# Adding up the weighted values of attention by accumulating on-chip transfers instead of VectorE additions

## The chip, the cores and the metric

One Trainium2 chip, of which the kernel uses one core. The metric is the device time of one execution in microseconds (us), as the median of several runs; lower is better.

## The reference

The input `x` has 2048 rows of 640 numbers (float32). Its layer norm `xn` goes two ways, and the two results are combined:

```python
qkv = xn @ wqkv                        # 32 heads of 20 columns, each with q, k, v
# sliding window: row s looks at rows s, s-2, ..., s-14 (8 places)
logits = einsum("bhsd,bhswd->bhsw", q, kg) * scale    # masked where the row would be below 0
attn = softmax(logits, axis=-1)
o = einsum("bhsw,bhswd->bhsd", attn, vg)              # the sum that the change is about
s = o @ wo
g = silu(((xn @ w_gate) * (xn @ w_up)) @ w_down)
return x + s * g
```

The weights of both ways are scaled by 8. What the change touches is the second `einsum`: for each row, eight value vectors are weighted by the softmax and added.

## The kernel before, in words

**Products in split form.** Every large product is computed by TensorE from operands that are split into a high and a low part (`mm3`, L95; `qkv`, L295), three products for one. Weights are split as they are needed: ScalarE writes the high part (L85), GpSimd writes the low part by a subtraction (L86, `split_wf` for the gate and up weights, `split_wq` for the q, k, v weights).

**Units.** Attention is cut into 12 units: six groups of heads (four of 5 heads, two of 6) times even and odd rows. A unit has eight column blocks of 128 rows. `qkv(u, i)` makes block i on TensorE and ScalarE copies it out of PSUM into the unit's `q` and `kv` tiles (L297, L298). Transfers then shift `kv` rows from partition to partition (`kv<-kv`, L302), so that all eight places of the window lie in the same partition as the row.

**Attention of a unit** (`attention`, a Python generator, L306) is nearly all VectorE work. For each of four pairs of window places: a product of q and k (L329) and a sum over the 20 columns of a head (L332). Then the softmax: mask, maximum, subtraction (L336 to L339), the exponential on ScalarE (L341), sum, reciprocal, product (L343 to L345). Then, for each of four pairs, a product of weights and values (`weighted`, L350), where the first goes to the tile `acc` and the other three go to `t` and are added to `acc` (L358). One last addition joins the two halves of a pair (L361) into the tile `o`, which is stored to memory (`o_scr`, L366).

**Pieces.** Between the units, TensorE works on pieces of the gate and up products: `gate_up(f, ch)` multiplies 128 columns f of both weights with 512 rows ch. A piece is 15 matmuls into a PSUM bank `g` and 15 into a bank `u`, two banks of each. ScalarE copies `g` to `gs` (L397). While any unit's attention is under way, VectorE multiplies `u` with `gs` into `hs` (L408), which frees the bank `u`; else ScalarE copies `u` (L410) and GpSimd multiplies (L411). `hs` is stored (`h_scr<-hs`, L412). The instruction L408 of a piece is put into the program after the first half of the next piece.

**What sets the order.** All instructions stand in a fixed order on each engine. Attention's steps are woven between TensorE's by a budget: each `yield` of the generator names what it costs VectorE in us, and `advance` takes steps until the budget that TensorE's work has granted is used up. A unit's attention can begin only when its last `qkv` has been issued. When no unit is under way, the budget is set to zero.

**Buffers.** `t` has two buffers, for products of q and k and for weighted values alike; `acc` is one of them too. `e` and `o` have one buffer each.

Of the kernel before, what the change touches and what calls it, by code (L numbers as in the profile page):

```python
# [14 lines left out]
ALU = mybir.AluOpType  # L15
# [4 lines left out]
P = 128  # L20
S, D, F = 2048, 640, 1536
H, DH = 32, 20
W, DIL = 8, 2
NT = S // P
NE = NT // DIL
# [15 lines left out]
PAIRS = range(0, W, 2)  # L41
# [9 lines left out]
def kernel(  # L51
# [11 lines left out]
    nc = tc.nc  # L63
# [68 lines left out]
    def load_x(s, n, t, cuts=(0, D)):  # L132
        j = tile_column(s)
        for c0, c1 in zip(cuts, cuts[1:]):
            nc.sync.dma_start(t[:, :, c0:c1], (xbv if s < NE else xv)[:, j:j + DIL * (n - 1) + 1:DIL, c0:c1])  # L135
        for i in range(n):
            xt[s + i] = t[:, i, :]
# [8 lines left out]
    load_x(4, 4, xc[:, 0:4])  # L146
    load_wf(1)
    load_x(8, 4, xc[:, 4:8])
    xd = st([P, 1, D], "o", 1)
    load_x(14, 1, xa[:, 2:3])  # L150
    load_x(15, 1, xd)
    ident = st([P, P], "ident", 1)
# [12 lines left out]
    o_scr = dr.tile([DIL, NQ, NE, P, QC], F32, name="o_scr")  # L165
# [98 lines left out]
    UN = [(g, r) for g in range(len(GROUPS)) for r in range(DIL)]  # L264
# [41 lines left out]
    def attention(u):  # L306
        g, r = UN[u]
        nh = GROUPS[g]
        c = nh * DH
        q, kv = q_t[u], kv_t[u]  # L310
        pair, one, small = [(n + 155) / 950 for n in (2 * NE * c, NE * c, NE * nh * W)]
        lg = st([P, NE * nh, W], "lg", 2)
        e = st([P, NE * nh, W], "e", 1)
        yield 1.0

        def places(a, j):

            y = kv[:, a, j:j + NE, :].rearrange("p i c -> p (i c)")
            return bass.AP(y.tensor, y.offset, [y.ap[0], [c, 2], y.ap[1]])

        def pair_tile():
            return st([P, 2, NE * c], "t", 2)

        def heads(y):
            return y.rearrange("p a (n d) -> p a n d", d=DH)

        for j in PAIRS:
            t = pair_tile()
            nc.vector.tensor_mul(t, q.rearrange("p i c -> p (i c)").unsqueeze(1).to_broadcast([P, 2, NE * c]),  # L329
                                 places(0, j))  # L330
            yield pair
            nc.vector.tensor_reduce(out=lg[:, :, j:j + 2].rearrange("p n a -> p a n"), in_=heads(t),  # L332
                                    op=ALU.add, axis=AX.X)
            yield pair
        m0 = lg[0:1].rearrange("p (i h) w -> p i h w", h=nh)
        nc.vector.tensor_add(m0, m0, mask.unsqueeze(2).to_broadcast([1, NE, nh, W]))  # L336
        sm = st([P, 2, NE * nh], "sm", 2)
        nc.vector.tensor_reduce(out=sm[:, 0, :], in_=lg, op=ALU.max, axis=AX.X)
        nc.vector.tensor_sub(lg, lg, sm[:, 0, :].unsqueeze(2).to_broadcast([P, NE * nh, W]))  # L339
        yield 3 * small  # L340
        nc.scalar.activation(e, lg, AF.Exp, scale=SCALE)  # L341
        yield small
        nc.vector.tensor_reduce(out=sm[:, 0, :], in_=e, op=ALU.add, axis=AX.X)  # L343
        nc.vector.reciprocal(sm[:, 1, :], sm[:, 0, :])
        nc.vector.tensor_mul(e, e, sm[:, 1, :].unsqueeze(2).to_broadcast([P, NE * nh, W]))  # L345
        yield 3 * small

        def weighted(j, t):
            pw = e[:, :, j:j + 2].rearrange("p n a -> p a n").unsqueeze(3).to_broadcast([P, 2, NE * nh, DH])
            nc.vector.tensor_mul(heads(t), pw, heads(places(1, j)))  # L350

        acc, t = pair_tile(), pair_tile()
        weighted(PAIRS[0], acc)
        yield pair
        for j in PAIRS[1:]:
            weighted(j, t)
            yield pair
            nc.vector.tensor_add(acc, acc, t)  # L358
            yield pair
        o = st([P, NE, c], "o", 1)  # L360
        nc.vector.tensor_add(o.rearrange("p i c -> p (i c)"), acc[:, 0, :], acc[:, 1, :])  # L361
        yield one
        for b in range(NQ):
            c0, c1 = max(GOFF[g], b * QC), min(GOFF[g] + c, (b + 1) * QC)
            if c0 < c1:
                nc.sync.dma_start(o_scr[r, b, :, :, c0 - b * QC:c1 - b * QC].rearrange("s p c -> p s c"),  # L366
                                  o[:, :, c0 - GOFF[g]:c1 - GOFF[g]])

    running = []

# [85 lines left out]
    def load_o(s, n, t):  # L456


        for b in range(NQ):
            nc.sync.dma_start(t[b * QB:(b + 1) * QB].rearrange("i n (q c) -> i (n q) c", c=QC),  # L460
                              o_scr[s // NE, b, s % NE:s % NE + n].rearrange("n (q i) c -> i (n q) c", i=QB))
        for i in range(n):
            o_t[s + i] = t[:, i]
# [24 lines left out]
    KH = KF // 2  # L488
# [21 lines left out]
    def sum_wd(k, part):  # L510
        r = wd_raw[k]
        if part == 0:
            v = wd_v[k] = {"B11": r[:, 0, 0], "B21": r[:, 1, 0], "B22": r[:, 1, 1]}
            v["T1"], v["T2"] = st([P, HALF], "lg", 2), st([P, HALF], "lg", 2)
            nc.vector.tensor_sub(v["T1"], r[:, 0, 1], r[:, 0, 0])
            nc.vector.tensor_sub(v["T2"], r[:, 1, 1], v["T1"])
        else:
            v = wd_v[k]
            v["T4"], v["T3"] = st([P, HALF], "e", 1), r[:, 0, 1]
            nc.vector.tensor_sub(v["T3"], r[:, 1, 1], r[:, 0, 1])  # L520
            nc.vector.tensor_sub(v["T4"], r[:, 1, 0], v["T2"])

# [8 lines left out]
    def load_h(n):  # L531

        a, b = 2 * n, 2 * n + 1
        if n % 2:
            ta, tb = st([P, KF, P], "t", 2), st([P, KF, P], "t", 2)
            nc.sync.dma_start(ta, h_scr[a])
            nc.sync.dma_start(tb, h_scr[b])
            h_raw[n] = {"A11": ta[:, :KH], "A12": ta[:, KH:], "A21": tb[:, :KH], "A22": tb[:, KH:]}
        else:
            h_raw[n] = {}  # L540
            for name, s, k, tag, m in (("A11", a, 0, "wraw", 3), ("A21", b, 0, "wraw", 3),
                                       ("A22", b, KH, "wraw", 3), ("A12", a, KH, "o", 1)):
                h_raw[n][name] = st([P, KH, P], tag, m)
                nc.sync.dma_start(h_raw[n][name], h_scr[s][:, k:k + KH])

# [63 lines left out]
    def gather(m):  # L609

        n, j = divmod(m, 7)
        a, b = 2 * n, 2 * n + 1
        p = bank["ACACABA"[j]]
        if j == 0:
            keep("M1", p, "lg", 2)
        elif j == 1:
            keep("M5", p, "lg", 2)
        elif j == 2:
            keep("U2", p, "e", 1)
        elif j == 3:  # L620
            g_t[a] = st([P, D], "q", 2)
            nc.vector.tensor_add(g_t[a][:, HALF:], kept["U2"], p)
            return lambda: silu(a, 1)
        elif j == 4:
            g_t[b] = st([P, D], "q", 2)
            nc.vector.tensor_add(g_t[b][:, HALF:], kept["M5"], p)
            return lambda: silu(b, 1)
        elif j == 5:
            nc.vector.tensor_add(g_t[a][:, :HALF], kept["M1"], p)
            return lambda: silu(a, 0)  # L630
        else:
            return lambda: silu(b, 0, p)
        return lambda: None
# [26 lines left out]
    nc.gpsimd.memset(mask, 0.0)  # L660
    for i in range(NE - 1):
        nc.gpsimd.memset(mask[:, i, :W - 1 - i], MASKED)
    sel = st([P, NQ, P], "sel", 1)
    nc.gpsimd.tensor_copy(sel.rearrange("p q (b i) -> p q b i", i=QB),
                          ident.rearrange("p (q i) -> p q i", i=QB).unsqueeze(2).to_broadcast([P, NQ, NQ, QB]))
    norm(4, 4)
# [82 lines left out]
    for ch in range(NCH):  # L749
        gate_up(f0, ch)  # L750
        if ch == 0:
# [3 lines left out]
            t = load_wo((4,))  # L755
    for ch in range(NCH):
        if ch == 3:
            load_wd(0)
            trans_o(0)
            load_o(1, 1, st([P, 1, D], "o", 1))  # L760
            load_o(2, 3, st([P, 3, D], "t", 2))
            load_o(5, 3, st([P, 3, D], "t", 2))
        gate_up(f1, ch)
        if ch < 3:
            for k in ((0, 1), (2, 3), (4,))[ch]:
                split_wo(k)
        if ch == 1:
            drain(len(UN) - 2)
            load_o(0, 1, t[:, 1:2])
        if ch == 2:  # L770
            advance(1e9)
# [24 lines left out]
    load_sx(0)  # L796
    load_sx(1)
    load_h(1)
    AHEAD = 4
    sum_h(1)  # L800
# [4 lines left out]
    for m in range(n_prod):  # L805
        n, j = divmod(m, 7)
# [61 lines left out]
```

## Time and profile before

| what | value |
|---|---|
| time, median of 3 runs | 787.05 us (786.82 to 787.56) |
| the profiled execution, first to last instruction | 786.0 us |
| TensorE matmul (PE) busy | 778.0 us, 99% |
| VectorE (DVE) busy | 659.3 us, 84% |
| ScalarE (ACT) busy | 234.2 us, 30% |
| GpSimd (POOL) busy | 147.9 us, 19% |
| granted TensorE clock, mean | 0.999 |

The profiled execution has no total of its own beside its span; the timed runs lie 1.05 us above that span. In the rows of the profile, PE is TensorE's matmuls and PEld its weight loads, DVE is VectorE, ACT ScalarE, POOL GpSimd, and SP the engine that issues transfers. "L329" is line 329 of the kernel. A row of a timeline gives start and duration in us, engine, line, operation, and output<-input tiles. "x2" counts merged instructions. A time in brackets is idle time of the engine before the row and who ended it.

### The profile page before, as it was taken

What the parts mean: (1) busy time and instruction counts of PE and PEld (TensorE: products, weight loads), DVE (VectorE), ACT (ScalarE), POOL (GpSimd) and SP (SyncE); (2) the same over time, 40 slices, a digit from 0 to 9 for tenths busy, and PEclk for the clock granted to TensorE, in tenths of its full rate; (3) what the DMA queues carried; (4) which work ended last, traced back from release to release, by engine and by line L of the source; (5) the groups of instructions that cost most, each with busy time, mean ns of one, the idle gap of its engine ahead of it and who ended that gap; (6) DMA issues with size and microseconds to landing.
All of it is one profiled execution on the core that took longest, in us unless ns stands there. A gap on an engine that the chain in (4) does not pass through costs nothing.

```text
span 786.0 us, 11222 instructions
## 1 busy us (share of the span) xinstructions
PE 778.0 (99%) x4454; PEld 708.9 (90%) x4454; DVE 659.3 (84%) x660; ACT 234.2 (30%) x536; POOL 147.9 (19%) x110
## 2 busy tenths in 40 slices
PE   8999999999999999999999999999999999999997
PEld 6889898888898898899898989888899999999997
DVE  6889899999999979996999999992177667777775
ACT  5334211121112111311221202012366564444442
POOL 5301211022013200410231000112467600000000
PEclk9999999999999999999999999999999999999999
DMA  8172122141132321404033131332797574555534
GB/s 321 67 230 75 42 61 72 48 123 48 50 83 89 95 71 61 117 28 112 28 105 86 58 86 58 107 103 66 160 274 209 170 270 131 206 200 188 182 101 135
DMA packets 81661, 92.68 MB, mean 118 GB/s; under 512 B 23032, under 2 KB 63304, under 8 KB 81480
## 3 DMA queue, kind: packets, MB, share of 16 engines
q1 hardware_dynamic: 81608, 91.96, 38.2%
q8 instruction: 35, 0.57, 0.3%
q14 instruction: 18, 0.15, 0.1%
HBM read 54.53 MB, written 28.31 MB: 105 GB/s over the span
## 4 chain that ended last, share of the span: by engine, by line
PE 97%; DMA 2%; ACT 1%; DVE 0%; SPq 0%; POOL 0%; issue 0%
PE q L295 26%; PE u L95 21%; PE g L95 21%; PE q L606 11%; PE q L95 9%; PE u L606 5%; PE g L606 3%; DMA wraw<-in_wgu 1%; DMA wraw<-in_wqkv 1%; PE q L229 0%; ACT wf L85 0%; SPq L135 0%; ACT wqh L85 0%; ACT xc L230 0%; POOL wql L86 0%; PE q L249 0%
## 5 line engine op out<-in xcount | busy, mean ns | idle before, releaser
L95 PE MATMUL u<-xc,wf 128*128 128x512 f32 (+1 forms) x735 | 176.2, 390 | 0.0
L95 PE MATMUL g<-xc,wf 128*128 128x512 f32 (+1 forms) x735 | 176.1, 390 | 0.0
L95 PEld LDWEIGHTS u<-xc,wf 128*128 128x128 f32 x735 | 135.7, 187 | 32.2
L95 PEld LDWEIGHTS g<-xc,wf 128*128 128x128 f32 x735 | 135.3, 187 | 31.0
L295 PE MATMUL q<-wqh,xc 128*128 128x300 f32 (+1 forms) x960 | 159.8, 309 | 2.1 <-DVE xc L231 1.2
L295 PEld LDWEIGHTS q<-wqh,xc 128*128 128x128 f32 x960 | 146.0, 188 | 4.3 <-DVE xc L231 1.5
L329 DVE TENSOR_TENSOR t<-q,kv 128x1600 f32<-128x1600 f32 (+1 forms) x48 | 97.9, 2040 | 10.1 <-DMA kv<-kv 10.1
L350 DVE TENSOR_TENSOR t<-e,kv 128x1600 f32<-128x1600 f32 (+1 forms) x48 | 97.5, 2051 | 1.1
L86 POOL TENSOR_TENSOR wf<-wraw,wf 128x256 fp32r<-128x256 f32 (+2 forms) x22 | 48.8, 2232 | 248.1 <-ACT wf L85 248.1
L332 DVE TENSOR_REDUCE lg<-t 128x80 f32<-128x1600 f32 (+1 forms) x48 | 92.6, 1930 | 1.2
L397 ACT ACTIVATE gs<-g 128x512 f32<-128x512 f32 x48 | 28.7, 598 | 205.9 <-PE g L95 197.2
L295 PE MATMUL q<-wql,xc 128*128 128x300 f32 (+1 forms) x480 | 86.3, 309 | 0.0
L358 DVE TENSOR_TENSOR t<-t,t 128x1600 f32<-128x1600 f32 (+1 forms) x36 | 80.2, 2228 | 1.1
L295 PEld LDWEIGHTS q<-wql,xc 128*128 128x128 f32 x480 | 74.4, 188 | 0.0
L297 ACT ACTIVATE kv<-q 128x200 f32<-128x200 f32 (+1 forms) x96 | 33.4, 348 | 129.4 <-PE q L295 129.4
L606 PE MATMUL q<-xc,wf 128*128 128x320 f32 x432 | 67.3, 309 | 0.0
L606 PEld LDWEIGHTS q<-xc,wf 128*128 128x128 f32 x432 | 64.3, 188 | 0.0
L86 POOL TENSOR_TENSOR wql<-wraw,wqh 128x300 fp32r<-128x300 f32 (+4 forms) x15 | 34.0, 2292 | 142.7 <-ACT wqh L85 142.7
L95 PE MATMUL q<-wf,wf 128*128 128x320 f32 x156 | 35.7, 310 | 0.0
L408 DVE TENSOR_TENSOR hs<-u,gs 128x512 f32<-128x512 f32 x39 | 26.6, 683 | 0.6 <-issue 0.6
L95 PEld LDWEIGHTS q<-wf,wf 128*128 128x128 f32 x156 | 26.1, 188 | 0.0
L86 DVE TENSOR_TENSOR wf<-ot,wf 128x640 fp32r<-128x640 f32 x13 | 15.5, 1190 | 11.9 <-ACT wf L85 11.9
(161 smaller groups left out, 888.9 us busy)
## 6 DMA issues: line engine op xcount, KB each, us to landing
h_scr<-hs SPq DMA_DIRECT2D x48, 256.0 KB, 2.3
wraw<-in_wgu SPq DMA_DIRECT2D x12, 640.0 KB, 4.9
t<-h_scr SPq DMA_DIRECT2D x8, 768.0 KB, 7.8
hs<-s_scr SPq DMA_DIRECT2D x16, 320.0 KB, 4.0
gs<-in_x SPq DMA_DIRECT2D x16, 320.0 KB, 4.4
wraw<-h_scr SPq DMA_DIRECT2D x12, 384.0 KB, 5.9
out<-q SPq DMA_DIRECT2D x14, 320.0 KB, 3.7
wraw<-in_wd SPq DMA_DIRECT2D x12, 320.0 KB, 4.8
```

The lines of the kernel that those rows point to most:

```text
L86: eng.tensor_sub(lo, raw, hi.bitcast(F32))
L95: nc.tensor.matmul(acc, a, b, start=first and n == 0, stop=last and n == len(runs) - 1)
L295: nc.tensor.matmul(p, xT[(r * NE + i) // TPC][a][:, k, t0:t0 + P], wq[g][b][:, k], start=n == 0, stop=n == len(runs) - 1, skip_group_check ...
L297: nc.scalar.activation(kv_t[u][:, :, W - 1 + i, :], p[:, c:].rearrange("p (a c) -> p a c", a=2), AF.Copy)
L329: nc.vector.tensor_mul(t, q.rearrange("p i c -> p (i c)").unsqueeze(1).to_broadcast([P, 2, NE * c]), places(0, j))
L332: nc.vector.tensor_reduce(out=lg[:, :, j:j + 2].rearrange("p n a -> p a n"), in_=heads(t), op=ALU.add, axis=AX.X)
L350: nc.vector.tensor_mul(heads(t), pw, heads(places(1, j)))
L358: nc.vector.tensor_add(acc, acc, t)
L397: nc.scalar.activation(gs, pp[0], AF.Copy)
L408: nc.vector.tensor_mul(hs, pp[1], gs)
L606: nc.tensor.matmul(p, y[:, i, k], wd_t[name][k][:, l], start=new and r == 0, stop=r == len(runs) - 1, skip_group_check=True)
```

## The change

In units 0 to 9 the three additions of `t` to `acc` (L358) go. In their place GpSimd issues an accumulating transfer for each: it reads `t` and `acc` in on-chip memory and writes their sum to `acc`. The last two units keep VectorE's additions. The last addition of the two halves and the store are put into a function `close`. In units 0 to 9 it is not called at the unit's end, but in the next unit's attention, after that unit's last product and sum of q and k. It works in place, so the tile `o` is gone.

The buffers change with it. The products of q and k, and the first of the three weighted products, use a new tile `l` with one buffer. The other two use `t`. `acc` gets one buffer of its own. `e` shares two buffers with `lg`. Tiles of other stages that borrowed `o`, `e` or `sel` now borrow `acc`, `l` or `ot`.

```diff
+        def pair_tile(tag="l", bufs=1):
+            return st([P, 2, NE * c], tag, bufs)
...
             nc.vector.tensor_reduce(out=lg[:, :, j:j + 2].rearrange("p n a -> p a n"), in_=heads(t),
                                     op=ALU.add, axis=AX.X)
             yield pair
+            if j == PAIRS[-1]:
+                close_unit()
...
-        acc, t = pair_tile(), pair_tile()
+        acc = pair_tile("acc", 1)
         weighted(PAIRS[0], acc)
         yield pair
         for j in PAIRS[1:]:
+            t = pair_tile() if j == PAIRS[1] else pair_tile("t", 2)
             weighted(j, t)
             yield pair
-            nc.vector.tensor_add(acc, acc, t)
-            yield pair
...
+            if u < len(UN) - DIL:
+                nc.gpsimd.dma_start(acc, t, accum_op=ALU.add)
+            else:
+                nc.vector.tensor_add(acc, acc, t)
+                yield pair
+
+        def close():
+            nc.vector.tensor_add(acc[:, 0, :], acc[:, 0, :], acc[:, 1, :])
+            o = acc[:, 0, :].rearrange("p (i c) -> p i c", c=c)
+            for b in range(NQ):
...
+                    nc.sync.dma_start(o_scr[r, b, :, :, c0 - b * QC:c1 - b * QC].rearrange("s p c -> p s c"),
+                                      o[:, :, c0 - GOFF[g]:c1 - GOFF[g]])
+
+        if u < len(UN) - DIL:
+            open_units.append(close)
+        else:
+            close()
+            yield one
```

In the rows of the program's order below, numbers at a tile's end name the allocation, not a buffer. After the change the lines below L330 have moved: L329 and L332 stay, L350 becomes L352, L361 becomes L368, L366 becomes L373, L408 becomes L428, L412 becomes L432. The accumulating transfers are L362.

First VectorE, from unit 1's weighted values into unit 2's products of q and k. `hs_1355` is the piece f = 2, ch = 0, and `hs_1396` the piece ch = 1. Before:

```order
L350 TENSOR_TENSOR t_1312<-e_1118,kv_757 128x1600
L350 TENSOR_TENSOR t_1313<-e_1118,kv_757 128x1600
L358 TENSOR_TENSOR t_1312<-t_1312,t_1313 128x1600
L408 TENSOR_TENSOR hs_1355<-u_1291,gs_1307 128x512
L350 TENSOR_TENSOR t_1313<-e_1118,kv_757 128x1600
L358 TENSOR_TENSOR t_1312<-t_1312,t_1313 128x1600
L350 TENSOR_TENSOR t_1313<-e_1118,kv_757 128x1600
L358 TENSOR_TENSOR t_1312<-t_1312,t_1313 128x1600
L408 TENSOR_TENSOR hs_1396<-u_1333,gs_1349 128x512
L361 TENSOR_TENSOR o_1399<-t_1312 128x800
L329 TENSOR_TENSOR t_1419<-q_1121,kv_163 128x1600
```

The same place after, where the same two pieces are `hs_1367` and `hs_1410`:

```order
L352 TENSOR_TENSOR acc_1254<-lg_1076,kv_757 128x1600
L352 TENSOR_TENSOR l_1274<-lg_1076,kv_757 128x1600
L352 TENSOR_TENSOR t_1297<-lg_1076,kv_757 128x1600
L352 TENSOR_TENSOR t_1321<-lg_1076,kv_757 128x1600
L329 TENSOR_TENSOR l_1341<-q_1126,kv_163 128x1600
L332 TENSOR_REDUCE lg_1324<-l_1341 128x2x40
L428 TENSOR_TENSOR hs_1367<-u_1302,gs_1318 128x512
L329 TENSOR_TENSOR l_1370<-q_1126,kv_163 128x1600
L332 TENSOR_REDUCE lg_1324<-l_1370 128x2x40
L329 TENSOR_TENSOR l_1388<-q_1126,kv_163 128x1600
L332 TENSOR_REDUCE lg_1324<-l_1388 128x2x40
L428 TENSOR_TENSOR hs_1410<-u_1345,gs_1361 128x512
```

Both `hs` products have moved back: from among unit 1's additions to behind the first product of q and k of unit 2, which writes the one buffer of `l` that the first transfer of unit 1 reads.

Next GpSimd, over units 0 and 1. `wf_1073` and `wf_1352` are the low parts of the weights f = 2 and f = 3. Before:

```order
L86 TENSOR_TENSOR wql_939<-wraw_811,wqh_938 128x900
L86 TENSOR_TENSOR wql_939<-wraw_813,wqh_938 128x600
L86 TENSOR_TENSOR wf_1073<-wraw_522,wf_1072 128x1280
L86 TENSOR_TENSOR wf_1352<-wraw_1288,wf_1351 128x1280
L86 TENSOR_TENSOR wql_1639<-wraw_1508,wqh_1638 128x900
```

After, where the same low parts are `wf_1080` and `wf_1364`:

```order
L86 TENSOR_TENSOR wql_939<-wraw_813,wqh_938 128x600
L362 DMA acc_1027<-l_1029 128x1600
L362 DMA acc_1027<-t_1054 128x1600
L362 DMA acc_1027<-t_1057 128x1600
L86 TENSOR_TENSOR wf_1080<-wraw_522,wf_1079 128x1280
L362 DMA acc_1254<-l_1274 128x1600
L362 DMA acc_1254<-t_1297 128x1600
L362 DMA acc_1254<-t_1321 128x1600
L86 TENSOR_TENSOR wf_1364<-wraw_1299,wf_1363 128x1280
```

Each low part now stands behind the three transfers of a unit. A transfer waits for VectorE's product and for the landing of the transfer before it, and GpSimd waits with it.

Last SP, around the store of unit 0. `kv_163` are the shifts for unit 2. Before:

```order
L412 DMA h_scr<-hs_1050 128x4x128
L412 DMA h_scr<-hs_1095 128x4x128
L366 DMA o_scr<-o_1099 128x8x100
L412 DMA h_scr<-hs_1159 128x4x128
L302 DMA kv_163<-kv_163 112x2x400
L302 DMA kv_163<-kv_163 15x2x400
```

After:

```order
L432 DMA h_scr<-hs_1050 128x4x128
L432 DMA h_scr<-hs_1102 128x4x128
L432 DMA h_scr<-hs_1164 128x4x128
L373 DMA o_scr<-acc_1027 128x8x100
L302 DMA kv_163<-kv_163 112x2x400
L302 DMA kv_163<-kv_163 15x2x400
```

The store has moved behind one more store of `hs`, directly ahead of unit 2's shifts, and it waits for unit 0's `close`, which is now in unit 1's attention.

More of the change, by code (lines that the diff above doesn't have):

```diff
@@ L148 @@
     load_x(8, 4, xc[:, 4:8])
-    xd = st([P, 1, D], "o", 1)
+    xd = st([P, 1, D], "acc", 1)
     load_x(14, 1, xa[:, 2:3])
@@ L312, in attention @@
         lg = st([P, NE * nh, W], "lg", 2)
-        e = st([P, NE * nh, W], "e", 1)
+        e = st([P, NE * nh, W], "lg", 2)
         yield 1.0
@@ L319, in places @@
             return bass.AP(y.tensor, y.offset, [y.ap[0], [c, 2], y.ap[1]])
-        def pair_tile():
-            return st([P, 2, NE * c], "t", 2)
+        def pair_tile(tag="l", bufs=1):
+            return st([P, 2, NE * c], tag, bufs)
         def heads(y):
@@ L355, in attention, with close_unit @@
         for j in PAIRS[1:]:
+            t = pair_tile() if j == PAIRS[1] else pair_tile("t", 2)
             weighted(j, t)
             yield pair
-            nc.vector.tensor_add(acc, acc, t)
-            yield pair
[L360 to L367, printed above, removed]
+            if u < len(UN) - DIL:
[7 more added lines that the diff above has]
+            for b in range(NQ):
+                c0, c1 = max(GOFF[g], b * QC), min(GOFF[g] + c, (b + 1) * QC)
+                if c0 < c1:
+                    nc.sync.dma_start(o_scr[r, b, :, :, c0 - b * QC:c1 - b * QC].rearrange("s p c -> p s c"),
[5 more added lines that the diff above has]
+            yield one
+    open_units = []
+    def close_unit():
+        while open_units:
+            open_units.pop(0)()
     running = []
@@ L518, in sum_wd @@
             v = wd_v[k]
-            v["T4"], v["T3"] = st([P, HALF], "e", 1), r[:, 0, 1]
+            v["T4"], v["T3"] = st([P, HALF], "acc", 1), r[:, 0, 1]
             nc.vector.tensor_sub(v["T3"], r[:, 1, 1], r[:, 0, 1])
@@ L541, in load_h @@
             for name, s, k, tag, m in (("A11", a, 0, "wraw", 3), ("A21", b, 0, "wraw", 3),
-                                       ("A22", b, KH, "wraw", 3), ("A12", a, KH, "o", 1)):
+                                       ("A22", b, KH, "wraw", 3), ("A12", a, KH, "l", 1)):
                 h_raw[n][name] = st([P, KH, P], tag, m)
@@ L618, in gather @@
         elif j == 2:
-            keep("U2", p, "e", 1)
+            keep("U2", p, "acc", 1)
         elif j == 3:
@@ L662 @@
         nc.gpsimd.memset(mask[:, i, :W - 1 - i], MASKED)
-    sel = st([P, NQ, P], "sel", 1)
+    sel = st([P, NQ, P], "ot", 2)
     nc.gpsimd.tensor_copy(sel.rearrange("p q (b i) -> p q b i", i=QB),
@@ L759 @@
             trans_o(0)
-            load_o(1, 1, st([P, 1, D], "o", 1))
+            load_o(1, 1, st([P, 1, D], "l", 1))
             load_o(2, 3, st([P, 3, D], "t", 2))
```

## The prediction

> **What bounds the kernel now.** I read the page's busy times, then TensorE's waits, then the windows of the attention stage, and last the timelines of TensorE and VectorE where they meet.
>
> ```profile
> PE 778.0 (99%) x4454; PEld 708.9 (90%) x4454; DVE 659.3 (84%) x660; ACT 234.2 (30%) x536; POOL 147.9 (19%) x110
> PE 97%; DMA 2%; ACT 1%; DVE 0%; SPq 0%; POOL 0%; issue 0%
> PE q L157 <- POOL ident masks.py:199: 1.4, 1, 1.4
> PE q L295 <- DVE xc L231: 1.2, 1, 1.2
> PE q L295 <- ACT xc L230: 0.9, 2, 0.6
> PEld q L295 <- ACT wqh L85: 0.2, 1, 0.2
> PEld q L295 <- ACT q L298: 0.2, 1, 0.2
> 105.00:149.40 44.40, 44.40 (x241) 38.90 (x240) 43.32 (x33) 7.77 (x22) 4.17 (x1) 1.00 0.25 74
> 186.90:224.60 37.70, 37.70 (x213) 33.40 (x212) 36.65 (x30) 6.96 (x21) 0.28 (x1) 1.00 0.27 69
> ```
>
> TensorE is busy 99% and is 97% of the chain that ended last. Its waits, as far as the list names who ended them, are a few us, nearly all on the normalised input at the start (L157, L230, L231); the two entries of 0.2 us are all that attention's stage costs it. The windows (columns: span, PE, PEld, DVE, ACT, POOL, clock, DMA share, GB/s) show TensorE busy for the whole of each stretch, VectorE for 43.3 of 44.4 and 36.65 of 37.7 us. So VectorE is nearly full, yet nobody waits for it. Work taken from it cannot shorten the kernel; the change can at most add waits to TensorE. Whatever TensorE loses in this stage is added to the end in full, since it never has a pause to make it up in.
>
> **What goes.** Thirty additions leave VectorE:
>
> ```profile
> L358 DVE TENSOR_TENSOR t<-t,t 128x1600 f32<-128x1600 f32 x24 | 52.1, 2170 | 0.7
> L358 DVE TENSOR_TENSOR t<-t,t 128x1920 f32<-128x1920 f32 x12 | 28.1, 2343 | 0.4
> ```
>
> 24 x 2.17 + 6 x 2.34 = 66 us, about 6.6 us a unit. All of it lies beside TensorE's work: gain 0.
>
> **What comes, the transfers.** No accumulating transfer is in the trace. One moves 128 x 1600 x 4 bytes = 800 KB, and reads a second 800 KB, the destination. Call X the time from the end of VectorE's product to the landing. The nearest rows (columns: KB, us from issue to landing):
>
> ```profile
> wraw<-in_wgu SPq DMA_DIRECT2D x12, 640.0 KB, 4.9
> ...
> kv<-kv SPq DMA_DIRECT2D x8, 262.5 KB, 3.0
> ...
> kv<-kv SPq DMA_DIRECT2D x4, 420.0 KB, 3.7
> o_scr<-o SPq DMA_DIRECT2D x4, 400.0 KB, 3.6
> ...
> xc<-in_x SPq DMA_DIRECT2D x1, 1280.0 KB, 10.7
> xc<-in_xq SPq DMA_DIRECT2D x1, 1280.0 KB, 6.9
> ```
>
> Between on-chip buffers 157.5 KB more cost 0.7 us, so 800 KB moved once would land in 3.7 + 380 x 0.7/157.5 = 5.4 us. From memory, 640 KB more cost 2.0 us, and 800 KB come out at 4.9 + 0.5 = 5.4 as well. A whole second pass at the flatter of the two slopes adds 2.5: 7.9. I take X = 7.5, near two passes, since reading is doubled and writing is not. GpSimd's issue lies inside X. The ends kept for the range are 4.9 (the 640 KB row) and 10.7 (the slower 1280 KB row).
>
> The Trainium skill (Collectives: The Full Stack, "The bandwidth ceiling") says that an add in the transfer engines is slow because it reads two sources, which halves a copy's rate. By that the whole second pass counts, X = 7.9 (an estimate), and the sum below would be 0.8 us more; no run so far shows it.
>
> **Where a transfer is waited for.** The first transfer of a unit reads `l`, and the next unit's first product (L329) writes the same buffer. In most units that product must wait for the next unit's `qkv` anyway, and VectorE, with 36.65 - 6.6 = 30 of 37.7 us left to do, has 7.7 us for a wait of X - 3.7. Only units 1 and 2 follow directly, since units 0 and 1 begin close together. There VectorE is this busy:
>
> ```profile
> 91.46 3.56 DVE L350 TENSOR_TENSOR t<-e,kv 128x1600 f32<-128x1600 f32 x2
> 94.94 0.68 DVE L408 TENSOR_TENSOR hs<-u,gs 128x512 f32<-128x512 f32 x1
> 95.54 1.82 DVE L358 TENSOR_TENSOR t<-t,t 128x1600 f32<-128x1600 f32 x1
> ...
> 99.25 4.49 DVE L358 TENSOR_TENSOR t<-t,t 128x1600 f32<-128x1600 f32 x1
> ...
> 107.96 0.99 DVE L361 TENSOR_TENSOR o<-t 128x800 f32<-128x800 f32 x1
> 108.87 1.82 DVE L329 TENSOR_TENSOR t<-q,kv 128x1600 f32<-128x1600 f32 x1
> ...
> 123.93 0.48 DVE L336 TENSOR_TENSOR lg<-lg,mask 1x320 f32<-1x320 f32 x1
> ...
> 127.48 3.56 DVE L350 TENSOR_TENSOR t<-e,kv 128x1600 f32<-128x1600 f32 x2
> ...
> 132.82 0.68 DVE L408 TENSOR_TENSOR hs<-u,gs 128x512 f32<-128x512 f32 x1
> ...
> 144.87 1.82 DVE L329 TENSOR_TENSOR t<-q,kv 128x1600 f32<-128x1600 f32 x1
> 146.72 1.82 DVE L332 TENSOR_REDUCE lg<-t 128x80 f32<-128x1600 f32 x1
> 148.46 0.68 DVE L408 TENSOR_TENSOR hs<-u,gs 128x512 f32<-128x512 f32 x1
> ```
>
> And GpSimd's low parts, and TensorE's groups that need the banks:
>
> ```profile
> 98.19 3.86 POOL L86 TENSOR_TENSOR wf<-wraw,wf 128x1280 fp32r<-128x1280 f32 x1 [14.30 <-ACT wf L85]
> ...
> 224.32 2.95 POOL L86 TENSOR_TENSOR wf<-wraw,wf 128x1280 fp32r<-128x1280 f32 x1 [41.68 <-ACT wf L85]
> ```
>
> ```profile
> 121.29 3.66 PE L95 MATMUL g<-xc,wf 128*128 128x512 f32 x15
> 124.78 3.66 PE L95 MATMUL u<-xc,wf 128*128 128x512 f32 x15
> ...
> 131.78 3.67 PE L95 MATMUL u<-xc,wf 128*128 128x512 f32 x15
> ...
> 138.78 3.66 PE L95 MATMUL u<-xc,wf 128*128 128x512 f32 x15
> ...
> 145.78 3.67 PE L95 MATMUL u<-xc,wf 128*128 128x512 f32 x15
> 149.28 0.85 PE L295 MATMUL q<-wqh,xc 128*128 128x300 f32 x5
> ```
>
> The order is unchanged up to unit 0's second product, which ends at 91.46 + 3.56 = 95.0. The two others end at 95.54 + 2 x 1.85 = 99.2. Then, in the new order:
>
> 1. Unit 1's first product waits for the landing: 95.0 + X (a wait of X - 4.2).
> 2. Products and sums of unit 1 took 123.93 - 108.87 = 15.1, and hold one more `hs` now (0.6): 15.7. The `close` takes 0.9 (107.96 to 108.87). Softmax and two weighted products: 131.0 - 123.9 = 7.1. `acc` must be stored before it is written again; the store lands in 3.6 against the 3.55 of the softmax, with its issue some 0.3 more. Unit 1's second product ends at 95.0 + X + 24.0 = 119.0 + X.
> 3. Unit 2's first product waits again for X: 119.0 + 2X. The `hs` of ch = 0 ends 4.3 later (144.87 to 149.14): 123.3 + 2X.
> 4. A low part on GpSimd and VectorE's products hinder each other: the one at 98.19 made an addition of 1.82 last 4.49, 2.7 lost. In the new order it starts after the third transfer's issue, at about 95.0 + 2X, among unit 1's products and sums. If it meets a product, 2.7 go; if it starts with a sum, 2.95 - 1.85 = 1.1 go. I take 1.9: 125.2 + 2X.
> 5. The `hs` of ch = 1 comes 6.0 later (two products, one sum, itself), and the low part of f = 3, at 119.0 + 3X or so, costs another 1.9: 133.1 + 2X.
>
> TensorE's group at 138.78 reuses the bank of 124.78, and needs ch = 0 done: X up to 6.8. The group at 145.78 reuses that of 131.78, and needs ch = 1: X up to 6.35. Before, the first had 138.78 - 133.50 = 5.3 us to spare. So TensorE waits **2X - 12.7**, at X = 7.5 **2.3 us**, once. In all other pieces VectorE's lag is less than before.
>
> **What else is behind the new waits.** GpSimd stands still until its transfers are issued; queued behind are the low parts. That of f = 2 would end by 95 + 2X + 4 = 114, and is needed ten matmuls after 121.29, at 123.6: covered by 9.6 us. That of f = 3 ends by 146 and isn't needed until unit 3's products, which begin at 149.28, are done. SP's store of unit 0 waits for `close`, at 95.0 + X + 17.6 = 120; behind it are unit 2's shifts, needed at 119.0 + 2X = 134, with 3.7 to land: covered by 10. The other moved buffers are written long after their last use: 0.
>
> Sum: 786.0 + 2.3 = 788.3 for the span; with the 1.05 us by which the timed runs lie above it, **789.4 us**, 0.3% slower.
>
> **The rivals.** About 0.2% (1.6 us) is what a measurement of this kernel can tell from no change.
>
> *Forecast, 0.43:* X from 7.15 to 8.8, TensorE waits 1.6 to 4.9 us: 788.7 to 792.0.
>
> *No change, 0.41:* X under 7.15. VectorE's waits for `l` are taken from the 5.3 us to spare, and TensorE loses under 1.6 us; at X = 6.35 or less 787.1. For it: one pass alone gives 5.4, and both low parts might meet sums. Against it: the second read. The Trainium skill (DMA: Bandwidth & Descriptors, "Anatomy of one DMA") fits a transfer issued by GpSimd as 2.0 us plus bytes over 436 GB/s, which is an estimate of 3.9 us for one pass and speaks for this rival; the 640 KB row, at 4.9, lies above it.
>
> *Transfers much slower, 0.12:* X over 8.8. If GpSimd can't write a transfer's descriptors while VectorE runs a product, each issue waits for up to 1.82, and X is 9.3. Then unit 0's third transfer lands at 95.0 + 3X = 122.9, after `close` is ready at 95.0 + X + 17.6 = 121.9: 5.9 + 1.0 = 6.9 us, 794.0; at X = 10.1 it is 10.1 us and 797. The 4.49 us addition shows that the two do block each other; that descriptors suffer, no row shows. The Trainium skill (SBUF — State Buffer, "Who interferes with whom") has this trap for VectorE's two-port modes and infers that two-input products don't cause it, hence the low chance.
>
> *Faster, 0.04:* it would take the 2.1 us of waits on L230 and L231 at the start, 785.0. Only buffers of a few tiles change there.
>
> Together: slower 0.43 + 0.12 = 0.55, same 0.41, faster 0.04. The range runs from 786.5, where a run without any wait may fall, to 797, X = 10.1; the forecast's own is 788.7 to 792.0.
>
> **What would show it.** VectorE waiting for a transfer ahead of L329 twice, near 99 and 126 us, for X - 4 each, and little elsewhere. TensorE waiting for VectorE's `hs` once or twice between 138 and 155 us and not after. Accumulating transfers landing in about 7.5 us, GpSimd idle most of that. VectorE's busy time down by about 66 us. Wrong would be: TensorE's waits at later units, behind ScalarE's exponential or a late low part; a first transfer landing in under 6.5 us with a slower kernel, or in over 8 without one.

## The result, and the profile after

The changed kernel takes 807.22 us (median of 4 runs, 805.54 to 808.93) against 787.13 us (786.82 to 787.56): a ratio of 1.0251, with a 95% interval of 1.0239 to 1.0264. That is slower, as forecast, but 20 us slower and not 2.3, and far outside the range of 786.5 to 797. The profiled execution of the changed kernel is the slowest of its four (808.93 us); its span is 807.2 us, 21.2 more than the 786.0 before.

First the page of the changed kernel: busy times, the chain that ended last, and one group (busy us, mean ns of one | idle time ahead of them, and what ended it).

```profile
PE 783.6 (97%) x4454; PEld 711.1 (88%) x4454; DVE 603.3 (75%) x629; ACT 234.1 (29%) x537; POOL 164.2 (20%) x141
...
PE 56%; DVE 20%; issue 7%; DMA 4%; SPq 1%; ACT 1%; DVEq 0%; ACTq 0%
...
L329 DVE TENSOR_TENSOR l<-q,kv 128x1600 f32<-128x1600 f32 (+1 forms) x48 | 116.5, 2427 | 88.9 <-DMA kv<-kv 61.4
```

VectorE has 56 us less to do (659.3 before), and still it is now on the chain: TensorE's share fell from 97% to 56%. VectorE stands idle for 61 us ahead of the first product of q and k, for `kv` shifts (10.1 us before). That wait is not a loss in itself, as a run below shows which has most of it and loses nothing; what counts is what stands behind it in VectorE's queue.

The waits of TensorE and of VectorE in the changed kernel (us in total, times, longest):

```profile
PE u L95 <- DVE hs L428: 13.6, 6, 6.2
```

```profile
DVE l L329 <- DMA kv<-kv: 61.4, 6, 21.1
...
DVE l L329 <- issue: 6.0, 2, 3.0
```

TensorE waits six times for VectorE's `hs`, where the prediction had one such wait. The two waits of VectorE of 3.0 us that the profile puts down to "issue" are the ones for `l`.

The distances between the starts of TensorE's groups (3.50 us where nothing waits) account for 20.5 of the 21.2 us in the profiled execution:

| place | lost us |
|---|---|
| units 1 and 2, 139 to 155 us: waits 0.5 and 3.46, then a slow group 1.65 | 5.6 |
| unit 6, 320 to 325 us: wait 6.37, then a slow group 1.89 | 8.3 |
| `hs` waits at 190, 276 and 545 us: 1.64, 1.75, 0.85 | 4.2 |
| `qkv` of three units, beginning at 194, 233 and 363 us: 1.12, 0.66, 0.63 | 2.4 |

The transfers (KB, median us from issue to landing):

```profile
acc<-t POOLq DMA_DIRECT2D x16, 800.0 KB, 6.0
...
wraw<-in_wgu SPq DMA_DIRECT2D x12, 640.0 KB, 6.4
acc<-l POOLq DMA_DIRECT2D x8, 800.0 KB, 7.4
...
kv<-kv SPq DMA_DIRECT2D x8, 350.0 KB, 7.8
...
kv<-kv SPq DMA_DIRECT2D x4, 420.0 KB, 5.4
```

An accumulating transfer of 800 KB lands in 6.0 to 7.4 us, by the medians of the two groups. Other transfers beside them became slower: weights 4.9 before, the 420 KB shifts 3.7, and the 350 KB shifts 3.6 us.

Now VectorE where the prediction had its wait, in the changed kernel's timeline:

```profile
92.93 1.82 DVE L352 TENSOR_TENSOR l<-lg,kv 128x1600 f32<-128x1600 f32 x1
...
101.80 1.82 DVE L329 TENSOR_TENSOR l<-q,kv 128x1600 f32<-128x1600 f32 x1 [2.99 <-issue]
...
109.71 4.53 DVE L329 TENSOR_TENSOR l<-q,kv 128x1600 f32<-128x1600 f32 x1
...
126.41 1.82 DVE L352 TENSOR_TENSOR l<-lg,kv 128x1600 f32<-128x1600 f32 x1
...
134.67 1.83 DVE L329 TENSOR_TENSOR l<-q,kv 128x1600 f32<-128x1600 f32 x1 [2.97 <-issue]
...
138.27 0.68 DVE L428 TENSOR_TENSOR hs<-u,gs 128x512 f32<-128x512 f32 x1
138.87 1.81 DVE L329 TENSOR_TENSOR l<-q,kv 128x1600 f32<-128x1600 f32 x1
140.72 1.82 DVE L332 TENSOR_REDUCE lg<-l 128x80 f32<-128x1600 f32 x1
142.57 4.47 DVE L329 TENSOR_TENSOR l<-q,kv 128x1600 f32<-128x1600 f32 x1
147.08 1.82 DVE L332 TENSOR_REDUCE lg<-l 128x80 f32<-128x1600 f32 x1
148.82 0.68 DVE L428 TENSOR_TENSOR hs<-u,gs 128x512 f32<-128x512 f32 x1
```

Unit 0's second product ends at 94.75 and unit 1's at 128.23; the next writes of `l` start at 101.80 and 134.67. So X is 7.05 and 6.44 us. The `hs` of ch = 1 ends at 149.50, and the bank that it frees is taken at once. TensorE at that place, and its granted clock there (span, then PE, PEld, DVE, ACT, POOL, clock, DMA share, GB/s):

```profile
149.55 5.31 PE L95 MATMUL u<-xc,wf 128*128 128x512 f32 x15 [3.29 <-DVE hs L428]
```

```profile
149.50:155.00 5.50, 5.45 (x18) 4.39 (x19) 5.40 (x6) 0.60 (x1) 0.00 (x0) 0.69 0.17 51
```

After the wait the clock is 0.69 and the group lasts 5.31 in place of 3.66 us. This wait cost more than its length.

The largest loss lies at 320 us and was in no part of the prediction. GpSimd, SyncE, VectorE and TensorE there, each from its timeline:

```profile
303.99 0.86 POOL L362 DMA_DIRECT2D acc<-t  x1 [7.03 <-DMA acc<-t]
304.55 1.62 POOL L431 TENSOR_TENSOR hs<-hs,gs 128x512 f32<-128x512 f32 x1
```

```profile
287.56 19.00 SPq L432 DMA_DIRECT2D h_scr<-hs  x2
306.66 5.39 SPq L302 DMA_DIRECT2D kv<-kv  x4
```

```profile
313.81 1.82 DVE L329 TENSOR_TENSOR l<-q,kv 128x1600 f32<-128x1600 f32 x1 [21.07 <-DMA kv<-kv]
...
319.27 0.68 DVE L428 TENSOR_TENSOR hs<-u,gs 128x512 f32<-128x512 f32 x1
```

```profile
320.01 5.55 PE L95 MATMUL u<-xc,wf 128*128 128x512 f32 x15 [6.21 <-DVE hs L428]
```

Unit 5 has run out of steps sooner, since its transfers are not charged to the budget. So a piece is finished while no unit is "running", and its `hs` goes to GpSimd (L431). There it stands behind unit 5's third transfer, which waits for the second to land. Its store stands in SyncE's queue ahead of unit 6's shifts. The shifts go at 306.7, VectorE idles 21 us, and TensorE waits for an `hs` that VectorE has behind its first products of unit 6.

### The profile page after: what moved, and what is told of

It reads as the page before. It is cut to its first block, busy times and chain, and to the rows that moved or that the text cites. A ratio compares the mean times of both kernels' runs of the same rounds, so it can differ in the third digit from the quotient of the medians.

```text
span 807.2 us, 11273 instructions
## 1 busy us (share of the span) xinstructions
PE 783.6 (97%) x4454; PEld 711.1 (88%) x4454; DVE 603.3 (75%) x629; ACT 234.1 (29%) x537; POOL 164.2 (20%) x141
## 4 chain that ended last, share of the span: by engine, by line
PE 56%; DVE 20%; issue 7%; DMA 4%; SPq 1%; ACT 1%; DVEq 0%; ACTq 0%
PE q L295 14%; PE q L626 10%; PE q L95 9%; PE u L95 8%; DVE l L329 7%; PE g L95 6%; DVE lg L332 6%; PE u L626 5%; DMA kv<-kv 3%; PE g L626 3%; DVE hs L428 2%; SPq L302 1%; DVE t L352 1%; DVE acc L364 1%; DVE l L352 1%
## 5 line engine op out<-in xcount | busy, mean ns | idle before, releaser
L95 PE MATMUL u<-xc,wf 128*128 128x512 f32 (+1 forms) x735 | 180.2, 397 | 13.6 <-DVE hs L428 13.6
L329 DVE TENSOR_TENSOR l<-q,kv 128x1600 f32<-128x1600 f32 (+1 forms) x48 | 116.5, 2427 | 88.9 <-DMA kv<-kv 61.4
L332 DVE TENSOR_REDUCE lg<-l 128x80 f32<-128x1600 f32 (+1 forms) x48 | 92.6, 1929 | 1.1
L86 POOL TENSOR_TENSOR wf<-wraw,wf 128x256 fp32r<-128x256 f32 (+2 forms) x22 | 44.9, 2057 | 76.3 <-ACT wf L85 54.0
L362 POOL DMA_DIRECT2D acc<-t x20 | 17.2, 860 | 144.3 <-DMA acc<-l 73.3
L352 DVE TENSOR_TENSOR t<-lg,kv 128x1600 f32<-128x1600 f32 (+1 forms) x24 | 45.5, 1928 | 0.0
L362 POOL DMA_DIRECT2D acc<-l x10 | 8.9, 886 | 158.0 <-DVE l L352 158.0
L86 POOL TENSOR_TENSOR wql<-wraw,wqh 128x300 fp32r<-128x300 f32 (+4 forms) x15 | 28.2, 1942 | 20.1 <-ACT wqh L85 20.1
L343 ACT ACTIVATE lg<-lg 128x320 f32<-128x320 f32 (+1 forms) x12 | 5.9, 490 | 88.8 <-DVE lg L341 88.7
L352 DVE TENSOR_TENSOR acc<-lg,kv 128x1600 f32<-128x1600 f32 (+1 forms) x12 | 28.0, 2333 | 4.5 <-DMA o_scr<-acc 4.2
```

What stands on the lines that cost most here:

```text
L86: eng.tensor_sub(lo, raw, hi.bitcast(F32))
L95: nc.tensor.matmul(acc, a, b, start=first and n == 0, stop=last and n == len(runs) - 1)
L362: nc.gpsimd.dma_start(acc, t, accum_op=ALU.add)
```

## The experiments

Two theories stood against each other. *The prediction's:* all is the wait for `l` in units 1 and 2. *The order's:* the transfers cost nothing in the planner's budget, so the next unit's work is put into the queues too early, and late `hs` products and late shifts follow. Runs of the kernel before beside these had medians of 787.64 to 787.99 us. Where a row below is a timeline, it is told which kernel it is of.

**Units 2 to 9 alone, and units 0 and 1 alone.** The other units add with VectorE.

```diff
-            if u < len(UN) - DIL:
+            if 2 <= u < len(UN) - DIL:
...
-        if u < len(UN) - DIL:
+        if 2 <= u < len(UN) - DIL:
```

> Units 0 and 1 add with VectorE again; units 2 to 9 keep their transfers. The prediction's theory (TensorE loses only where units 1 and 2 wait for the one buffer of l): that place is gone, 787 to 788 us. The theory read from the profile after (VectorE stands at the next unit's first product until the shifts of kv have landed, with the hs products queued behind it): only the 5 to 6 us lost between 138 and 155 us go, and 13 to 15 us stay: 800 to 803 us.

Measured: 802.66 us, ratio 1.0181 (1.0158 to 1.0203). The kernel with transfers in units 2 to 9 alone, TensorE's waits:

```profile
PE u L95 <- DVE hs L428: 7.2, 3, 5.7
PE q L295 <- ACT q L298: 3.5, 1, 3.5
```

The stretch from 139 to 155 us is clean, the loss at unit 6 is there in full (5.90 + 2.44 us). A second kind of wait shows: `qkv` waits 3.5 us for ScalarE, where the copies of q and kv out of PSUM stand behind an exponential that VectorE's late sums hold back. The prediction's theory cannot be the whole.

For units 0 and 1 alone, the same two lines become:

```diff
-            if u < len(UN) - DIL:
+            if u < 2:
```

> Only units 0 and 1 use transfers; units 2 to 9 add with VectorE. The prediction's theory, if it stood for the whole loss: about 807 us. The theory of the late shifts: only the loss between 138 and 155 us is left, about 5 us with the slower clock behind the wait: 791 to 793 us, and TensorE waits for no hs after 155 us.

Measured: 802.27 us, ratio 1.0186 (1.0171 to 1.0201). The wait for `l` costs what it cost in the changed kernel (0.52 + 3.51 + 1.65 = 5.7 us). But another 7.5 us are lost later, in units that add with VectorE as before, which neither theory had. SyncE and VectorE in units 0 and 1 alone, where the largest of them arises:

```profile
245.08 1.60 SPq L302 DMA_DIRECT2D kv<-kv  x2
256.55 0.38 SPq L373 DMA_DIRECT2D o_scr<-acc  x1
257.03 1.59 SPq L302 DMA_DIRECT2D kv<-kv  x2
```

```profile
260.92 1.83 DVE L329 TENSOR_TENSOR l<-q,kv 128x1600 f32<-128x1600 f32 x1 [4.40 <-DMA kv<-kv]
```

The store of unit 4's sum stands between unit 5's two pairs of shifts, and waits for the sum. SyncE at that place in the kernel before:

```profile
237.55 5.51 SPq L302 DMA_DIRECT2D kv<-kv  x4
255.37 0.38 SPq L366 DMA_DIRECT2D o_scr<-o  x1
```

There the four shifts left together, 18 us ahead of that store. The order of the whole program has moved because of two units.

**The transfers left out, and the transfers charged.**

```diff
-                nc.gpsimd.dma_start(acc, t, accum_op=ALU.add)
+                pass
```

> The thirty transfers aren't issued, so the three weighted products of units 0 to 9 are not added to the first; everything else stands as after the change, the order and the budget too. If the shorter budget and the moved instructions alone cost the time: over 800 us. If it is the transfers (the wait for l, shared transfer engines that make the shifts of kv land late, GpSimd held up): 787 to 790 us, with kv landing in 3 to 4 us as before.

This kernel leaves three of the four weighted products out of the sum. Measured: 787.77 us, ratio 1.0002 (0.9993 to 1.0011). The changed order, without transfers, costs nothing. GpSimd in this kernel:

```profile
273.79 2.83 POOL L431 TENSOR_TENSOR hs<-hs,gs 128x512 f32<-128x512 f32 x1 [3.47 <-ACT hs L430]
```

The `hs` product of unit 5 is on GpSimd here as well, and harmless with no transfer ahead of it.

```diff
                 nc.gpsimd.dma_start(acc, t, accum_op=ALU.add)
+                yield pair
```

> Transfers as after the change, but each is charged to the budget as the addition was, so that the next unit's products are woven in as late as before. If the loss in units 3 to 9 is that the hs products stand behind a first product that waits for kv: most of the 14 us there go, the wait for l stays: 790 to 796 us. If it is the transfers alone, whatever the order: 803 to 808 us.

Measured: 788.01 us, ratio 1.0010 (1.0001 to 1.0019). Its landings:

```profile
acc<-t POOLq DMA_DIRECT2D x16, 800.0 KB, 6.2
acc<-l POOLq DMA_DIRECT2D x8, 800.0 KB, 6.3
...
kv<-kv SPq DMA_DIRECT2D x8, 350.0 KB, 4.5
```

The same transfers (the 24 of 800 KB) land in 6.2 to 6.3 us by the medians, and the loss is 0.1%. VectorE's wait for the shifts in this kernel:

```profile
DVE l L329 <- DMA kv<-kv: 50.8, 7, 11.9
```

VectorE waits nearly as long here (61.4 us in the changed kernel), and it costs nothing. One line, which tells the planner that a transfer takes as long as an addition, brings back 19 us. So it takes both: transfers of 6 to 7 us, and an order that is planned as if they took none.

**One `hs` product.** It goes to VectorE instead of GpSimd while a unit's sum is still open.

```diff
-            if running:
+            if running or open_units:
```

> One hs product, the one that closes a piece while no attention unit is under way, is computed by VectorE instead of GpSimd; all else is the changed kernel. Theory of the queue: that product stands on GpSimd behind unit 5's third transfer (which waited 7.0 us for the second), its store in SyncE's queue stands ahead of unit 6's kv shifts, and VectorE then waits 21.1 us for them; the whole 6.4 + 1.9 us of TensorE at 320 us goes, and the kernel takes about 799 us (797 to 801), with no wait of TensorE over 1 us between 280 and 330 us. Rival, that the shifts are late there because the transfers slow them on the way: the shifts are issued earlier but land late, the wait at 320 us shrinks by less than half, 803 to 807 us.

Measured: 799.32 us, ratio 1.0141 (1.0124 to 1.0158); no wait is left between 199 and 532 us. The chain at 320 us is shown: one product moved, and the wait is gone. The medians differ by 807.2 - 799.3, about 8 us, close to the 8.3 of the account. But the two profiled executions differ elsewhere too. VectorE's first product of unit 3, in the changed kernel and then in this one:

```profile
179.50 5.66 DVE L329 TENSOR_TENSOR l<-q,kv 128x1600 f32<-128x1600 f32 x1 [14.38 <-DMA kv<-kv]
```

```profile
180.07 8.48 DVE L329 TENSOR_TENSOR l<-q,kv 128x1600 f32<-128x1600 f32 x1 [13.56 <-DMA kv<-kv]
```

The order of the instructions is the same up to here. The product meets GpSimd's low parts, which had stood behind unit 2's third transfer, and lasts 5.66 or 8.48 us instead of 1.82. TensorE then loses 1.64 us in the one execution and 4.65 + 1.64 in the other, while the small losses between 200 and 500 us are gone from the second. So the loss at one place varies from execution to execution, and that 7.9 and 8.3 agree so well is in part chance.

**The shifts from ScalarE's queue.** First alone, then with the other repair.

```diff
-                    nc.sync.dma_start(kv_t[u][p0 + 1:p1 + 1, :, i0 - 1:i1 - 1, :],
+                    nc.scalar.dma_start(kv_t[u][p0 + 1:p1 + 1, :, i0 - 1:i1 - 1, :],
```

> The kv shifts are issued from ScalarE's queue, behind the evictions that they read, instead of from SyncE's; all else is the changed kernel. Theory of the queue (stores in SyncE's queue that wait for hs or for a sum hold back the shifts behind them): the 8.3 us at 320 us fall below 3, the small losses between 190 and 280 us (5.2 us in all) halve, the 5.6 us of units 1 and 2 stay: 795 to 800 us. Rival, that shifts are late because transfers slow them on the way: they land as late as before whichever queue issues them, 804 to 808 us.

Measured: 803.36 us (798.42 to 804.87), ratio 1.0188 (1.0154 to 1.0221), between the two expectations. The profiled execution is the fastest of the four, 798.42 us; where the others lose 4.6 to 6.5 us more, no trace shows. ScalarE's queue ahead of unit 6:

```profile
293.32 2.12 ACTq L302 DMA_DIRECT2D kv<-kv  x2
```

The last shifts go at 293 us and no longer behind the store (306.7 in the changed kernel), and the wait of TensorE at unit 6 is gone in this execution. That the shifts stood behind a store is a link of that chain.

> Both repairs at once: the hs product on VectorE and the kv shifts from ScalarE's queue. If the losses are of separate places, what is left is the wait for l in units 1 and 2, 5.7 us, and up to 3 us of small ones: 793 to 797 us. If the two repairs only shift one shortage of VectorE's time from place to place, it stays at the 799 us of the one.

Measured: 800.91 us, ratio 1.0172 (1.0140 to 1.0203). Both repairs bring no more than the `hs` product alone (799.32). So nothing shows SyncE's queue as a cause of its own: it is the way by which the late product held back the shifts of unit 6, and moving the shifts takes nothing off what is left.

> Both repairs, and transfers in units 2 to 9 alone, without a charge. If the three causes (the wait for l in units 1 and 2, the hs product on GpSimd, the shifts behind stores) are the whole loss, 787 to 790 us, as before the change. If a shortage is left that only the charge to the budget removes, 792 us or more.

Measured: 795.89 us (793.20 to 797.47), ratio 1.0098 (1.0074 to 1.0121). With units 0 and 1 on VectorE as well, some 8 us stay. The profiled execution, the fastest, shows an `hs` wait in unit 5 with a slow group behind it (2.49 + 1.62 us) and `qkv` behind ScalarE (1.16).

**Half transfers.** Each adds one of the two planes.

```diff
-                nc.gpsimd.dma_start(acc, t, accum_op=ALU.add)
+                nc.gpsimd.dma_start(acc[:, 0, :], t[:, 0, :], accum_op=ALU.add)
```

> Each transfer adds only the first of the two planes of a product, 400 of 800 KB; the second plane of three of the four products is left out of the sum in units 0 to 9. The order of the instructions is the changed kernel's. Theory that the length of the transfer sets the losses: landings fall from 6.0 to 7.4 us to about 4, each wait for l from 3.0 to under 1, the third transfer of unit 5 is issued about 3 us sooner, shifts land within a us of the kernel before; half or more of the 20 us goes, 790 to 798 us. Rival, that the order of the instructions is to blame whatever the transfers last: 802 to 807 us.

Measured: 793.21 us (789.38 to 796.47), ratio 1.0064 (1.0038 to 1.0090). The landings with half transfers:

```profile
acc<-t POOLq DMA_DIRECT2D x16, 400.0 KB, 4.4
acc<-l POOLq DMA_DIRECT2D x8, 400.0 KB, 5.5
```

Landings fall by 1.6 to 1.9 us, less than expected, and 14 of the 20 us go. The losses grow much faster than the length of a transfer.

**Where the charge is needed.** First transfers in units 0 and 1 alone, charged: `if u < 2` in both places, and `yield pair` behind the transfer.

> Transfers in units 0 and 1 alone, as in the run before of these two units, but each transfer is charged to the piece's budget like the addition that it replaces; units 2 to 11 add with VectorE. Theory of the plan (the missing charge makes units 1 and 2, and all that follow them, enter the pieces earlier, and this is what the run without the charge lost, 7.5 us of it in units that add with VectorE): both the 5.7 us at 139 to 155 us and the later losses go, 787 to 789 us. Rival, that the tiles (one tile of l, one sum tile, the sum closed in the next unit) cost in units that add with VectorE: the later losses stay, 793 to 797 us. Third, that the wait for l costs at the 150 us group whatever the plan: at least 791 us.

Measured: 787.81 us, ratio 1.0000 (0.9991 to 1.0009). The later 7.5 us of units 0 and 1 alone came from the plan, and not from the tiles or the late `close`. VectorE's wait list of this kernel:

```profile
DVE l L329 <- issue: 2.4, 1, 2.4
```

One wait for `l` is still there and costs nothing. Next, transfers in ten units, with the charge in the first two alone:

```diff
                 nc.gpsimd.dma_start(acc, t, accum_op=ALU.add)
+                if u < 2:
+                    yield pair
```

> The changed kernel with transfers in ten units, charged to the budget in units 0 and 1 and not in units 2 to 9. Theory that the plan of the early units sets what follows: no wait of TensorE, 787 to 789 us. Theory that every uncharged unit enters the pieces too early by itself: the wait for l at 139 to 155 us is gone, the losses between 180 and 330 us are those of the run with transfers in units 2 to 9 (1.2, 5.3 and 8.4 us), 799 to 804 us.

Measured: 796.41 us (795.6 to 801.82), ratio 1.0130 (1.0092 to 1.0167), between the two expectations. TensorE's waits:

```profile
PE u L95 <- DVE hs L430: 5.6, 1, 5.6
```

One wait is left, at 308 us, and it is that of the `hs` product on GpSimd. Last, the same with `if running or open_units`, which puts that product on VectorE:

> The changed kernel with the transfers of units 0 and 1 charged to the budget and the one hs product on VectorE instead of GpSimd; transfers in ten units, eight of them without a charge. If the whole loss has these two causes, no wait of TensorE over 0.5 us is left and the time is that before the change, 787 to 789 us. If the uncharged units 2 to 9 cost anything of themselves, 791 us or more.

Measured: 788.09 us (787.43 to 789.20, 11 runs), ratio 1.0006 (0.9997 to 1.0016). The page, TensorE's waits and VectorE's timeline of this kernel:

```profile
PE 777.5 (99%) x4454; PEld 708.8 (90%) x4454; DVE 593.1 (75%) x630; ACT 234.3 (30%) x536; POOL 165.3 (21%) x140
```

```profile
PE q L157 <- POOL ident masks.py:199: 1.4, 1, 1.4
PE q L295 <- DVE xc L231: 0.9, 1, 0.9
PE q L295 <- ACT xc L230: 0.9, 2, 0.6
```

```profile
128.23 0.68 DVE L430 TENSOR_TENSOR hs<-u,gs 128x512 f32<-128x512 f32 x1
...
134.72 0.69 DVE L430 TENSOR_TENSOR hs<-u,gs 128x512 f32<-128x512 f32 x1 [4.07 <-issue]
135.32 2.38 DVE L329 TENSOR_TENSOR l<-q,kv 128x1600 f32<-128x1600 f32 x1
```

Thirty transfers in ten units, VectorE's work down by 66 us, and no loss. The last fence shows how: with the charge the `hs` of ch = 0 (128.23) and of ch = 1 (134.72) stand ahead of unit 2's first product, not behind it, so a late transfer holds back attention and not TensorE's bank. In the changed kernel they came at 138.27 and 148.82.

No version beats the kernel before. TensorE is busy for 777.5 of 785.7 us in the last, as it was before (778.0 of 786.0).

## Why the prediction was wrong

**What bounds the kernel, and the gain of 0: right.** In the last experiment 66.2 us fewer on VectorE (659.3 to 593.1) gain nothing. In the changed kernel itself only 56 of the forecast 66 us went. An addition that met nothing took 1.82 us, or 2.15 for the larger form; thirty of them are 24 x 1.82 + 6 x 2.15 = 57 us. The 66 had in it additions that met GpSimd's low parts and took longer (4.49 us at 99.25); in the changed kernel products meet them in their place.

**X: nearly right.** 7.05 and 6.44 us against 7.5. It lies between one pass (5.4) and two (7.9). The rule of the Trainium skill (Collectives: The Full Stack, "The bandwidth ceiling"), stated there for collectives, is that an add reads two sources; the estimate of 7.9 by that rule is 0.9 and 1.5 above the two measured X. By the prediction's own bound (X under 7.15) the rival of no change should have come. That it didn't is due to the next points; that the direction came out as forecast is luck as far as this sum goes.

**Where `l` is waited for: right.** VectorE waits twice, at 98.8 and 131.7 us, and TensorE waits between 138 and 155 us.

**"2X − 12.7": too small.** With the measured X it gives 0.8 us; the two waits came to 4.0 (0.5 and 3.46). Both low parts hit a product (4.53 and 4.47 us, 2.7 and 2.65 lost, where I took 1.9 for each): 1.6 us. And step 5 counts "two products, one sum, itself", where the order that is quoted ahead of the prediction has two products and two sums: 1.85 us. That was a plain miscount. With both put right the sum is 4.2.

**The price of a wait: wrong.** I took a wait at its length. TensorE's group after it ran at a clock of 0.69 and took 1.65 us more; the one at unit 6 took 1.89 more.

**"In all other pieces VectorE's lag is less than before": wrong, and the largest error.** It compares sums of work (30 of 37.7 us) and not the order. 14.9 of the 20.5 us lie there; the prediction had named waits at later units as a sign that it was wrong. The charged kernel shows the reason: the same work with the same transfers, in an order planned with their cost, loses nothing. The sentence that the next product "must wait for the next unit's `qkv` anyway, and VectorE has 7.7 us for a wait" overlooked that `hs` products stand behind that product in VectorE's queue. A wait there becomes one for TensorE as soon as it outlasts what the bank has to spare, whatever the sum of work leaves.

**"GpSimd stands still … queued behind are the low parts": incomplete.** An `hs` product was queued behind them, at one place in the program, put there by the rule on units under way (`running`), which the change touches without naming it. It cost about 8 us. The low parts were not harmless either: released late, they met a product of unit 3 (5.66 us instead of 1.82, at 179.5), just ahead of TensorE's wait at 190 us. The prediction read the order around units 0 to 2 and not at unit 6. The stores that hold back shifts in SyncE's queue were likewise priced at unit 2 alone, and it was at unit 6 that one came late.

**The rival of slow transfers: fell.** GpSimd's issues of transfers took 0.85 to 1.01 us each, also where VectorE's products ran (at 102.17 and 128.53 us). The Trainium skill (SBUF — State Buffer, "Who interferes with whom") infers for two-input products that they don't keep GpSimd from writing descriptors, and the trace agrees. Both measured X are well under the rival's 8.8 us; later transfers took up to 10.5 from issue to landing.

**What stays open.** The smaller losses from 180 us on come and go with small changes of order: 6.6 us in the changed kernel, 7.5 with units 0 and 1 alone, 5.4 with both repairs, 0 once the first two units are charged and the `hs` product is moved. In the changed kernel unit 3's shifts leave at 167.2 us and VectorE waits for them until 179.5; in the last experiment they leave at 159.3 and it starts at 169.7. How much of that is the early delay carried on, how much slow shifts beside transfers, and how much the low parts that meet a product, wasn't taken apart. Nor is it shown that the two causes of the last experiment are the whole loss in any order: with units 0 and 1 on VectorE, the `hs` product moved and the shifts on ScalarE's queue, some 8 us stayed, and no run has the same with the shifts left on SyncE's.

## What to carry to other kernels

Where a planner weaves work by costs, moving work to another engine changes the order of everything behind it: give the moved step a cost that stands for its length, even if the engine that the budget speaks of no longer does it. An engine with spare time still delays the bound if a product that others need stands in its queue behind one that waits; so compare queue positions, on every engine that may get the work and at every unit, before sums of work. A wait of the bounding engine is priced with the slow stretch that may follow it.

## What the runs showed of the hardware

**An accumulating transfer between on-chip buffers**, 800 KB: 6.0 to 7.4 us from issue to landing, as medians of the two groups in the changed kernel; 400 KB in the run with half transfers: 4.4 to 5.5. Halving the bytes saves about a quarter. All thirty of the changed kernel (six are of 960 KB) took 5.8 to 10.5 us, 6.6 in the middle. An issue holds GpSimd for 0.85 to 1.01 us.

**It slows its neighbours.** A shift of 350 KB on SyncE's queue took 7.8 us in the changed kernel, 4.2 in the same order with the transfers left out, 4.5 with charged transfers, and 3.6 before. Where it went from ScalarE's queue it took 3.6 beside the transfers too, but the shifts of 262.5 KB then took 6.6 (3.0 before), so not all of them are slowed alike; what decides it is not shown.

**TensorE after a pause.** In the changed kernel the groups after waits of 3.29 and 6.21 us took 5.31 and 5.55 us instead of 3.66, and those after waits of up to 1.6 us took 3.75 or 3.76. But it is no fixed bound. TensorE with the one `hs` product moved, and then with both repairs (the granted clock was 1.00 over the first group and 0.68 over the second):

```profile
150.68 3.76 PE L95 MATMUL u<-xc,wf 128*128 128x512 f32 x15 [3.33 <-DVE hs L428]
```

```profile
191.09 5.31 PE L95 MATMUL u<-xc,wf 128*128 128x512 f32 x15 [1.76 <-DVE hs L428]
```

A wait of 3.33 us left the clock alone, and one of 1.76 us was followed by a slow group. The Trainium skill (TensorE: Matmul & The Clock Gate, "Part 1: The HAM clock gate") tells of a clock that halves after an idle window of about 3.4 us and comes back after a busy one of that length. Half of 3.4 us is an estimate of 1.7 for the price of one slow stretch. The slow groups of these runs lost 1.6 to 2.4 us (1.65 at 149.55 us in the changed kernel). That a pause must be as long as the window, they do not show: a wait of 1.76 us was enough here, and one of 2.33 with transfers in units 2 to 9 and both repairs.
